# Raw weight tiles of the attention part are issued by GpSimd instead of SyncE

## The chip, the core and the metric

The kernel runs on one of the eight cores of a Trainium2 chip. A core has five engines with instruction queues of their own: TensorE (PE) for matrix products, VectorE (DVE), ScalarE (ACT), GpSimd (POOL), and SyncE (SP), which here only issues transfers. Sixteen DMA engines move data between HBM and the on-chip memory. The metric is device time in microseconds (us) of one execution. Before the change the median of three runs is 503.27 us (502.56 to 503.57).

## The reference

Three parts follow one another, all in float32. B = 2, 12 heads, 448 positions, head size 64; 896 tokens with 768 columns.

```python
scores = q @ k.T / 8;  scores = where(mask, -1e9, scores)      # causal
attn = exp(scores - max) / (sum(exp(scores - max)) + 1e-9)
x = (attn @ v)              # laid out as 896 tokens x 768
h = maximum(maximum(x @ w1, x @ w2), x @ w3)                   # 768 x 768 each
x = h @ w_out                                                  # 768 x 768
g = s * relu(x @ w_in) ** 2 + b                                # 768 x 2048
out = g @ w_out2                                               # 2048 x 768
```

## The kernel before

**Number format.** TensorE multiplies in a reduced format. Every operand is therefore split in a high and a low part (HL for q and k, x, h and g for the activations, whi and wlo for the weights), and a product is three products.

**Weights.** All four weight matrices lie in HBM as 56 tiles of 128 rows by 768 values of 8 bytes (768 KB each). A raw tile (wraw) is asked for by `fetch_w` (line 125), into one of three buffers. It is decoded in stages: ScalarE reads its two halves ("high" and "low", lines 144 and 147), VectorE clamps, shifts, sets the sign and adds (lines 153 to 179), ScalarE rounds to whi (line 184), VectorE forms wlo (line 92). "sign" is the last reader of the raw tile. For tiles decoded behind the attention, "sign" also asks for the next raw tile; for the first four (`tiles`, NT_AHEAD = 4) it doesn't, so the raw tiles of the attention part are asked for by explicit calls in the steps.

**Attention.** Twelve pairs of heads are worked on in a pipeline of 14 steps (`step(s)`, s = 0 to 13). The order of the work is written out by hand, and each engine executes its instructions in that order. In step s, with new = s and old = s - 1:

- TensorE forms masks and scores of pair `new` (mask_a, mask_b, mask_c, scores; lines 350 to 388) in the banks A, B and C, transposes the exponentials of pair `old` (line 435), and multiplies pair s - 2 with v (pv, lines 451 to 460) into the one bank o.
- VectorE finds row minima (mx), ScalarE exponentials (p).
- The row sums of `old` are inverted, transposed by TensorE into a corner of bank A of the new pair (line 480), copied out by VectorE (rows, line 487), written to HBM by SyncE in two parts (rcd, lines 488 and 489) and read back as a broadcast in two halves (rb, line 497). The mask product of the next step writes bank A again, so it comes after the copy of rows.
- VectorE multiplies o with rb for pair s - 3 (xf, line 506). That empties bank o, and the next pv may begin. GpSimd makes x from xf (lines 296 and 92).
- q and k of pair s + 2 are split: VectorE casts (HL from R, line 309), GpSimd subtracts (HL, line 92) and copies the last columns (bd, line 296). R of pair s + 3 is scaled by GpSimd beforehand (`scaled`, line 296), and the cast needs that.
- SyncE loads R of pair s + 4 (line 268) and pieces of v (line 289): V_LOADS[s] gives how many ahead of the broadcast of rb and how many behind it.
- Raw weight tiles: the branch `else: fetch_w()` runs where there is no old pair, that is in steps 0 and 13, and `if s in FETCH` in steps 1, 4, 8, 10 and 11. Each is in SyncE's queue.

A transfer instruction waits in the queue of the engine that issues it, and what stands behind it in that queue waits too.

**After the attention** TensorE runs through the products of the other two parts (lines 698 and 807) while the weights are decoded ahead. The output is stored in two halves of the columns (line 825), seven stores each, in SyncE's queue between the last loads of raw tiles.

Of the kernel before, what the change touches and what calls it, by code (L numbers as in the profile page):

```python
# [26 lines left out]
FETCH = (1, 4, 8, 10, 11)  # L27
# [9 lines left out]
    12: ("hi2", "low3"),  # L37
}
V_GROUPS = ((0, 1), (1, 1), (2, 4), (6, 6))
V_LOADS = ((7, 7), (2, 5), (3, 4), (3, 0), (3, 0), (3, 0), (3, 0), (2, 0))  # L40
FILL = {12: (3, 5), 13: (0, 4)}
WARM = 10
BUSY = (7,)
# [7 lines left out]
def kernel(  # L51
# [14 lines left out]
    nc = tc.nc  # L66
# [55 lines left out]

    step = begin

    def fetch_w():
        if w_src:
            src = w_src.pop(0)
            raw = wr_p.tile([128, DM], I64, tag="wraw", name="wraw")
            nc.sync.dma_start(out=raw, in_=src)
            raws.append(raw)  # L130

    def decoder(over=None, fetch=fetch_w):


# [97 lines left out]
    def attention():  # L232
        with ExitStack() as c2:
# [52 lines left out]
            def load_v(n):  # L286
                for _ in range(min(n, len(v_list))):
                    to, of = v_list.pop(0)
                    nc.sync.dma_start(out=to, in_=of)  # L289
# [5 lines left out]
            def pool_scaled(out, in_, by):  # L295
                nc.gpsimd.tensor_scalar(
                    out=out, in0=in_, scalar1=by, scalar2=1.0, op0=ALU.mult, op1=ALU.mult
                )
# [4 lines left out]
            def scaled(p):  # L303
                q = pair[p]["R"][:, 0, :]
                pool_scaled(q, q, -scale)

            def split_hi(p):
                new_hl(p)
                nc.vector.tensor_copy(out=pair[p]["HL"][:, 0:4:2, :], in_=pair[p]["R"])  # L309

            def split_lo(p):
                HL, R = pair[p]["HL"], pair[p]["R"]
                for n in range(2):
                    sub_lo(nc.gpsimd, HL[:, 2 * n + 1], R[:, n], HL[:, 2 * n])
# [7 lines left out]
            def split_lo_early(p):  # L322
                HL, R = pair[p]["HL"], pair[p]["R"]
                nc.vector.scalar_tensor_tensor(
                    out=HL[:, 1], in0=R[:, 0], scalar=-scale, in1=HL[:, 0].bitcast(F32),
                    op0=ALU.mult, op1=ALU.subtract,
                )
                sub_lo(nc.vector, HL[:, 3], R[:, 1], HL[:, 2])
# [13 lines left out]
            def both_tails(p):  # L342
                HL = pair[p]["HL"].bitcast(F32)
                for h in range(2):
                    pool_scaled(bds[p % 3][hs[h], :, hs[h]], HL[hs[h], 0:2, TAIL:S], 1.0)
# [47 lines left out]
            def minima(p, i):  # L393
                e = pair[p]
                src, cols = (at(p, i), slice(2 * i, 2 * i + 2)) if i < NQ else (e["C"][:, 0:S], slice(2 * NQ, 2 * NQ + 1))
                nc.vector.tensor_reduce(
                    out=e["mx"][:, cols], in_=src, axis=mybir.AxisListType.X, op=ALU.min
                )
# [40 lines left out]
            def pt_copy(p, n, eng):  # L439
                copy = eng.copy if eng is nc.scalar else eng.tensor_copy  # L440
                copy(out=pair[p]["PT"][:, n * 512:(n + 1) * 512], in_=pair[p]["t", n])
# [50 lines left out]
            def broadcast(p):  # L492
                e = pair[p]
                flat = e["flat"]
                for h in range(2):
                    at = h * (NQ + 1) * 128
                    nc.sync.dma_start(
                        out=e["rb"][hs[h]], in_=flat[:, at:at + S].to_broadcast([D, S])
                    )
# [17 lines left out]
            for p in range(1, 4):  # L517
# [6 lines left out]
                out=tri.rearrange("p (a n) -> p a n", a=2), in_=tri.rearrange("p (a n) -> p a n", a=2), pattern=[[0, 2], [-1, TQ]], base=0, channel_multiplier=1,  # L524
# [26 lines left out]
            def step(s):  # L551
                new, old, out, nxt = (
                    p if 0 <= p < n_pairs else None for p in (s, s - 1, s - 2, s + 2)
                )
                loads = V_LOADS[s] if s < len(V_LOADS) else (0, 0)
                if new is not None:
# [31 lines left out]
                if new == 0:  # L588
                    for i in (0, 1, 2, NQ):
                        minima(new, i)  # L590
                    split_lo_early(1)
                    both_tails(1)
                    for n in (2, 3):
                        scaled(n)
                    for V in vs[:2]:
                        nc.gpsimd.memset(V[D:128, :, :, NQ, :], 0.0)
                elif new is not None:
                    minima(new, 2)
# [53 lines left out]
                if old is not None:  # L652
                    load_v(loads[0])
                    broadcast(old)
                else:
                    fetch_w()
                load_v(loads[1])
                if s in FETCH:
                    fetch_w()
                if s == LAST:  # L660
                    nc.sync.dma_start(out=sb[:, 0:1], in_=s2.to_broadcast([128, 1]))
                    nc.sync.dma_start(out=sb[:, 1:2], in_=b2.to_broadcast([128, 1]))
                if new == 1:
                    split_hi(nxt)
                    split_lo(nxt)
                    both_tails(nxt)
                    scaled(s + 3)
                if old is not None:
                    pt_copy(old, 2, nc.scalar)
                if new is not None:  # L670
# [11 lines left out]
            for s in range(n_pairs + 2):  # L682
                step(s)
# [196 lines left out]
```

## Time and profile before

| | us |
|---|---|
| median of three runs | 503.27 |
| profiled execution | 502.06 |
| its span in the trace | 500.3 |
| TensorE busy | 493.3 (99%) |
| VectorE busy | 340.5 (68%) |
| ScalarE busy | 282.9 (57%) |
| GpSimd busy | 71.4 (14%) |

The busy tenths in 40 slices of 12.5 us show where each engine works; GpSimd works in the attention part alone:

```profile
PE   8999999999999999999999999999999999999997
DVE  5778896665857667587677888888888644484401
ACT  5988977444445254444546878888786432253101
POOL 6988992300000000000000000000000000000000
DMA  5777534223324231333223323332333323261003
```

A share of the whole span says little about one stage: the 14% of GpSimd are 80% and more in slices 2 to 6. Issues of transfers aren't counted as busy. Every wait in the timelines carries, in brackets, how long the engine idled and what ended it.

### The profile page before, as it was taken

The numbers are of one execution on the slowest core, as the hardware profiler recorded it, in microseconds if no ns is written. First come the engines' busy times: TensorE is split into PE (matmuls) and PEld (weight loads), VectorE is DVE, ScalarE is ACT, GpSimd is POOL, SyncE is SP. The second block draws the span as 40 slices with busy tenths as digits, with TensorE's granted clock in tenths as the row PEclk, the third lists the DMA queues.
The fourth block names the chain that finished last, engine by engine and source line by source line (L and its number), as shares of the span: only waits on it lengthen the run. The fifth ranks groups of instructions, "written<-read, shape, count | busy, mean of one in ns | idle before, by whom it ended". The sixth has DMA issues, their size and how long they took to land.

```text
span 500.3 us, 7557 instructions
## 1 busy us (share of the span) xinstructions
PE 493.3 (99%) x2909; PEld 452.7 (90%) x2909; DVE 340.5 (68%) x512; ACT 282.9 (57%) x527; POOL 71.4 (14%) x103
## 2 busy tenths in 40 slices
PE   8999999999999999999999999999999999999997
PEld 4877888899999999999999999999999999999996
DVE  5778896665857667587677888888888644484401
ACT  5988977444445254444546878888786432253101
POOL 6988992300000000000000000000000000000000
PEclk9999999999999999999999999999999999999999
DMA  5777534223324231333223323332333323261003
GB/s 170 225 215 226 151 102 117 103 91 127 126 75 148 94 126 64 126 128 126 101 89 126 127 73 118 126 104 85 127 126 109 119 89 128 88 220 56 1 0 111
DMA packets 26212, 58.34 MB, mean 117 GB/s; under 512 B 13548, under 2 KB 17600, under 8 KB 26176
## 3 DMA queue, kind: packets, MB, share of 16 engines
q1 hardware_dynamic: 26032, 57.76, 35.2%
q8 instruction: 23, 0.38, 0.3%
q14 instruction: 13, 0.11, 0.1%
q10 hardware_dynamic: 144, 0.10, 0.1%
HBM read 55.05 MB, written 2.80 MB: 116 GB/s over the span
## 4 chain that ended last, share of the span: by engine, by line
PE 91%; DMA 2%; DVE 2%; SPq 2%; ACT 1%; POOL 1%; issue 0%; DVEq 0%; ACTq 0%
PE m L698 58%; PE m L807 23%; PE t L435 3%; PE o L451 2%; ACT p L408 1%; PE o L455 1%; SPq L289 1%; PE A L380 1%; PE C L388 1%; PE B L380 1%; DMA rcd<-rows 1%; DMA rb<-rcd 1%; DMA R<-in_qk_dram 1%; POOL HL L92 0%; PE o L460 0%
## 5 line engine op out<-in xcount | busy, mean ns | idle before, releaser
L698 PE MATMUL m<-x,whi 128*128 128x448 f32 x816 | 232.0, 366 | 0.0
L698 PEld LDWEIGHTS m<-x,whi 128*128 128x128 f32 x816 | 153.1, 188 | 12.3 <-ACT p L408 0.2
L698 PE MATMUL m<-x,wlo 128*128 128x448 f32 x408 | 149.0, 365 | 0.0
L807 PE MATMUL m<-whi,g 128*128 128x384 f32 x448 | 114.0, 334 | 0.0
L184 ACT CAST whi<-wa 128x768 fp32r<-128x768 f32 x56 | 46.7, 833 | 67.0 <-PE m L807 43.8
L698 PEld LDWEIGHTS m<-x,wlo 128*128 128x128 f32 x408 | 76.6, 188 | 6.0
L807 PEld LDWEIGHTS m<-whi,g 128*128 128x128 f32 x448 | 81.0, 188 | 0.0
L144 ACT ACTIVATE wa<-wraw 128x768 f32<-128x768 f32 x56 | 50.6, 904 | 52.3 <-DVE wlo L92 52.3
L92 DVE TENSOR_TENSOR wlo<-wa,whi 128x768 fp32r<-128x768 f32 x56 | 53.3, 953 | 38.4 <-ACT whi L184 38.4
L807 PE MATMUL m<-wlo,g 128*128 128x384 f32 x224 | 74.8, 334 | 0.0
L179 DVE CUSTOM_DVE_ANT_0 wa<-wa,wr 128x1536 uint16<-128x1536 uint16 x56 | 53.6, 957 | 1.9
L172 DVE SCALAR_TENSOR_TENSOR wa<-wraw,wa 128x768 int32<-128x768 int32 x56 | 53.7, 959 | 0.0
L147 ACT ACTIVATE wr<-wraw 128x768 int32<-128x768 uint32 x56 | 50.6, 904 | 0.0
L807 PEld LDWEIGHTS m<-wlo,g 128*128 128x128 f32 x224 | 42.0, 188 | 0.0
L705 DVE TENSOR_TENSOR t<-t,m 128x448 f32<-128x448 f32 x24 | 14.9, 621 | 38.7 <-PE m L698 38.7
L698 PE MATMUL m<-h,whi 128*128 128x448 f32 x144 | 40.9, 365 | 0.0
L166 DVE TENSOR_SCALAR wa<-wa 128x768 int32<-128x768 int32 x56 | 32.2, 575 | 1.8
L92 POOL TENSOR_TENSOR HL<-R,HL 128x448 fp32r<-128x448 f32 (+1 forms) x21 | 29.9, 1443 | 3.2 <-DVE HL L309 2.1
L792 ACT ACTIVATE r<-m 128x448 f32<-128x448 f32 x32 | 17.4, 544 | 22.2 <-PE m L698 22.2
L698 PEld LDWEIGHTS m<-h,whi 128*128 128x128 f32 x144 | 27.1, 188 | 2.1
L158 DVE TENSOR_SCALAR wa<-wa 128x768 f32<-128x768 f32 x52 | 28.7, 552 | 0.0
L781 DVE SCALAR_TENSOR_TENSOR r<-m,r 128x448 f32<-128x448 f32 x32 | 20.0, 625 | 12.3 <-ACT r L792 12.3
(85 smaller groups left out, 551.2 us busy)
## 6 DMA issues: line engine op xcount, KB each, us to landing
wraw<-in_w_dram SPq DMA_DIRECT2D x56, 768.0 KB
R<-in_qk_dram SPq DMA_DIRECT2D x11, 448.0 KB
rb<-rcd SPq DMA_DIRECT2D x24, 112.0 KB
out_dram<-o SPq DMA_DIRECT2D x13, 192.0 KB
v<-in_v_dram SPq DMA_DIRECT2D x4, 96.0 KB
v<-in_v_dram SPq DMA_DIRECT2D x2, 168.0 KB
v<-in_v_dram SPq DMA_DIRECT2D x6, 48.0 KB
v<-in_v_dram SPq DMA_DIRECT2D x2, 144.0 KB
```

The lines of the kernel that those rows point to most:

```text
L92: eng.tensor_tensor(out=lo, in0=full, in1=hi.bitcast(F32), op=ALU.subtract)
L144: nc.scalar.activation(out=e["f"], in_=e["high"].bitcast(F32), func=ACTF.Abs)
L147: nc.scalar.activation(out=e["r"], in_=e["low"].bitcast(U32), func=ACTF.Copy, scale=2.0 ** -29)
L158: nc.vector.tensor_scalar(out=e["f"], in0=e["f"], scalar1=UNDER, scalar2=OVER, op0=ALU.max, op1=ALU.min)
L166: nc.vector.tensor_scalar(out=a, in0=a, scalar1=3, scalar2=0x3FFFFFF8, op0=ALU.logical_shift_left, op1=ALU.bitwise_and,)
L172: nc.vector.scalar_tensor_tensor(out=e["a"], in0=e["high"], scalar=-0x40000000, in1=e["a"], op0=ALU.bitwise_and, op1=ALU.bitwise_or,)
L179: nc.vector.tensor_tensor(out=e["a"], in0=e["a"], in1=e["r"], op=ALU.add)
L184: nc.scalar.copy(out=e["hi"], in_=e["f"])
L698: nc.tensor.matmul(p, wt[w][:, ws], cols(act[i], a, b), start=(i == 0 and n == 0), stop=(i == len(act) - 1 and n == 2),)
L781: nc.vector.scalar_tensor_tensor(out=r, in0=p, scalar=0.0, in1=r, op0=ALU.max, op1=ALU.mult)
L792: after(0, lambda: nc.scalar.activation(out=r, in_=p, func=ACTF.Relu))
L807: nc.tensor.matmul(acc[t][:, 0:EH], gt[f][:, a, ts], w[:, ws], start=(f == 0 and n == 0), stop=(f == KG - 1 and n == 2),)
```

## The change

`fetch_w` takes the queue as an argument. In the attention part the raw tiles are now asked for in GpSimd's queue: in step 0 behind the scaling of pairs 2 and 3, in steps 1, 4, 8, 10 and 11 behind the step's own scaling. The branch that ran in steps 0 and 13 is gone, so that six raw tiles instead of seven are asked for in the steps. Of the v pieces behind rb one moves from step 2 to step 1: (2, 5), (3, 4) becomes (2, 6), (3, 3). "sign" goes on asking in SyncE's queue.

```diff
--- before.py
+++ after.py
@@ -37,7 +37,7 @@
     12: ("hi2", "low3"),
 }
 V_GROUPS = ((0, 1), (1, 1), (2, 4), (6, 6))
-V_LOADS = ((7, 7), (2, 5), (3, 4), (3, 0), (3, 0), (3, 0), (3, 0), (2, 0))
+V_LOADS = ((7, 7), (2, 6), (3, 3), (3, 0), (3, 0), (3, 0), (3, 0), (2, 0))
 FILL = {12: (3, 5), 13: (0, 4)}
 WARM = 10
 BUSY = (7,)
@@ -122,11 +122,11 @@
 
     step = begin
 
-    def fetch_w():
+    def fetch_w(queue=nc.sync):
         if w_src:
             src = w_src.pop(0)
             raw = wr_p.tile([128, DM], I64, tag="wraw", name="wraw")
-            nc.sync.dma_start(out=raw, in_=src)
+            queue.dma_start(out=raw, in_=src)
             raws.append(raw)
 
     def decoder(over=None, fetch=fetch_w):
@@ -592,6 +592,7 @@
                     both_tails(1)
                     for n in (2, 3):
                         scaled(n)
+                    fetch_w(nc.gpsimd)
                     for V in vs[:2]:
                         nc.gpsimd.memset(V[D:128, :, :, NQ, :], 0.0)
                 elif new is not None:
@@ -652,11 +653,7 @@
                 if old is not None:
                     load_v(loads[0])
                     broadcast(old)
-                else:
-                    fetch_w()
                 load_v(loads[1])
-                if s in FETCH:
-                    fetch_w()
                 if s == LAST:
                     nc.sync.dma_start(out=sb[:, 0:1], in_=s2.to_broadcast([128, 1]))
                     nc.sync.dma_start(out=sb[:, 1:2], in_=b2.to_broadcast([128, 1]))
@@ -665,6 +662,8 @@
                     split_lo(nxt)
                     both_tails(nxt)
                     scaled(s + 3)
+                if s in FETCH:
+                    fetch_w(nc.gpsimd)
                 if old is not None:
                     pt_copy(old, 2, nc.scalar)
                 if new is not None:
```

GpSimd's queue in steps 0 to 2, before: R is the scaling, HL the split, bd the copy of last columns, v a memset of v's unused rows.

```order
L296 TENSOR_SCALAR R<-R 128x448 x2
L596 MEMSET v_112 64x2x64
L596 MEMSET v_113 64x2x64
L92 TENSOR_TENSOR HL<-R,HL 128x448 x2
L296 TENSOR_SCALAR bd_109<-HL 64x2x64 x2
L606 MEMSET v_114 64x8x64
L606 MEMSET v_115 64x12x64
L92 TENSOR_TENSOR HL<-R,HL 128x448 x2
L296 TENSOR_SCALAR bd_107<-HL 64x2x64 x2
L296 TENSOR_SCALAR R<-R 128x448
L92 TENSOR_TENSOR HL<-R,HL 128x448 x2
```

The same place in the changed kernel:

```order
L296 TENSOR_SCALAR R<-R 128x448 x2
L129 DMA wraw<-in_w_dram 128x768
L597 MEMSET v_112 64x2x64
L597 MEMSET v_113 64x2x64
L92 TENSOR_TENSOR HL<-R,HL 128x448 x2
L296 TENSOR_SCALAR bd_109<-HL 64x2x64 x2
L607 MEMSET v_114 64x8x64
L607 MEMSET v_115 64x12x64
L92 TENSOR_TENSOR HL<-R,HL 128x448 x2
L296 TENSOR_SCALAR bd_107<-HL 64x2x64 x2
L296 TENSOR_SCALAR R<-R 128x448
L129 DMA wraw<-in_w_dram 128x768
```

A load now stands behind the scaling of pairs 2 and 3 and one behind the scaling of pair 4, each ahead of a split.

SyncE's queue in steps 1 to 3, before, from the first pieces of v behind the broadcast of step 1:

```order
L289 DMA v_114<-in_v_dram 16x4x64 x2
L289 DMA v_114<-in_v_dram 96x4x64 x2
L289 DMA v_114<-in_v_dram 32x4x64
L129 DMA wraw<-in_w_dram 128x768
L488 DMA rcd<-rows 7x128
L489 DMA rcd<-rows 1x64
L268 DMA R<-in_qk_dram 128x896
L289 DMA v_114<-in_v_dram 32x4x64
L289 DMA v_114<-in_v_dram 80x4x64 x2
L497 DMA rb<-rcd 64x448 x2
L289 DMA v_114<-in_v_dram 48x4x64 x2
L289 DMA v_114<-in_v_dram 64x4x64 x2
```

The same place in the changed kernel:

```order
L289 DMA v_114<-in_v_dram 16x4x64 x2
L289 DMA v_114<-in_v_dram 96x4x64 x2
L289 DMA v_114<-in_v_dram 32x4x64 x2
L488 DMA rcd<-rows 7x128
L489 DMA rcd<-rows 1x64
L268 DMA R<-in_qk_dram 128x896
L289 DMA v_114<-in_v_dram 80x4x64 x2
L289 DMA v_114<-in_v_dram 48x4x64
L497 DMA rb<-rcd 64x448 x2
L289 DMA v_114<-in_v_dram 48x4x64
L289 DMA v_114<-in_v_dram 64x4x64 x2
```

The raw tile ahead of rcd is gone, one piece of v (32 rows) has moved ahead of rcd, and three instead of four pieces stand between the broadcast of step 2 and the next rcd.

SyncE's queue at the end, before, from the last broadcast on (out_dram is the output):

```order
L497 DMA rb<-rcd 64x448 x2
L129 DMA wraw<-in_w_dram 128x768 x47
L825 DMA out_dram<-o 128x384 x7
L129 DMA wraw<-in_w_dram 128x768 x3
L825 DMA out_dram<-o 128x384 x6
L819 DMA out_dram<-o 128x192
```

The same place in the changed kernel:

```order
L497 DMA rb<-rcd 64x448 x2
L129 DMA wraw<-in_w_dram 128x768 x46
L824 DMA out_dram<-o 128x384 x7
L129 DMA wraw<-in_w_dram 128x768 x4
L824 DMA out_dram<-o 128x384 x6
L818 DMA out_dram<-o 128x192
```

One load, the 53rd of the 56, has moved behind the seven stores of the first half.

## Rows read from the trace of the kernel before

**Rows 1.** Busy by stretch: us, PE PEld DVE ACT POOL, clock, DMA share, GB/s.

```profile
21.88:28.26 6.38, 6.38 (x67) 5.31 (x66) 5.91 (x11) 6.27 (x21) 6.14 (x8) 1.00 0.86 256
28.26:35.86 7.60, 6.52 (x68) 5.36 (x66) 5.60 (x11) 6.22 (x20) 5.73 (x8) 1.00 0.57 146
35.86:43.10 7.24, 6.46 (x67) 5.33 (x65) 5.71 (x11) 6.21 (x20) 5.87 (x8) 1.00 0.92 222
43.10:49.49 6.39, 6.39 (x67) 5.32 (x65) 5.38 (x11) 6.05 (x20) 6.14 (x8) 1.00 0.74 238
```

**Rows 2.** Timeline of VectorE, products with rb: start, us, what, idle before.

```profile
32.21 0.62 DVE L506 TENSOR_TENSOR xf<-o,rb 128x448 f32<-128x448 f32 x1 [1.64 <-DMA rb<-rcd]
...
39.53 0.62 DVE L506 TENSOR_TENSOR xf<-o,rb 128x448 f32<-128x448 f32 x1 [1.33 <-DMA rb<-rcd]
```

**Rows 3.** Chain of waits, steps 2 and 3: start, us, what.

```profile
21.01 0.63 DVE HL L309
21.64 0.18 DVE rows L487
...
23.07 3.99 DMA rcd<-rows
...
28.89 1.78 SPq L289
```

**Rows 4.** Timeline of SyncE's DMA issues.

```profile
22.57 0.41 SPq L129 DMA_DIRECT2D wraw<-in_w_dram  x1
...
24.15 1.54 SPq L289 DMA_DIRECT2D v<-in_v_dram  x3
27.12 1.09 SPq L497 DMA_DIRECT2D rb<-rcd  x2
28.26 3.77 SPq L289 DMA_DIRECT2D v<-in_v_dram  x4
32.13 0.45 SPq L488 DMA_DIRECT2D rcd<-rows  x1
...
62.24 0.25 SPq L489 DMA_DIRECT2D rcd<-rows  x1
63.11 1.09 SPq L497 DMA_DIRECT2D rb<-rcd  x2
...
435.96 3.58 SPq L825 DMA_DIRECT2D out_dram<-o  x7
```

**Rows 5.** Timeline of GpSimd, steps 0 to 5, with idle time and its end.

```profile
11.03 1.09 POOL L296 TENSOR_SCALAR R<-R 128x448 f32<-128x448 f32 x2
...
20.41 0.56 POOL L296 TENSOR_SCALAR R<-R 128x448 f32<-128x448 f32 x1
21.79 3.03 POOL L92 TENSOR_TENSOR HL<-R,HL 128x448 fp32r<-128x448 f32 x2 [0.81 <-DVE HL L309]
...
32.92 0.56 POOL L296 TENSOR_SCALAR x<-xf 128x448 fp32r<-128x448 f32 x1 [1.00 <-DVE xf L506]
...
40.24 0.56 POOL L296 TENSOR_SCALAR x<-xf 128x448 fp32r<-128x448 f32 x1 [0.50 <-DVE xf L506]
...
42.66 3.05 POOL L92 TENSOR_TENSOR HL<-R,HL 128x448 fp32r<-128x448 f32 x2 [0.63 <-DVE HL L309]
...
46.42 0.56 POOL L296 TENSOR_SCALAR R<-R 128x448 f32<-128x448 f32 x1
```

**Rows 6.** Timeline of TensorE, first mask product of step 3.

```profile
21.88 0.27 PE L350 MATMUL A<-tri,identb 128*128 128x128 bf16 x2
```

**Rows 7.** Timeline of VectorE, step 6.

```profile
47.29 0.70 DVE L309 CAST HL<-R 128x896 fp32r<-128x896 f32 x1
48.82 0.28 DVE L487 COPY rows<-A 7x128 f32<-7x128 f32 x1 [0.83 <-PE A L480]
```

**Rows 8.** Timeline of ScalarE, second output half.

```profile
442.51 0.91 ACT L144 ACTIVATE wa<-wraw 128x768 f32<-128x768 f32 x1 [1.06 <-DVE wlo L92]
...
445.86 0.84 ACT L184 CAST whi<-wa 128x768 fp32r<-128x768 f32 x1 [1.63 <-PE m L807]
```

## Prediction

> **What bounds the kernel now.** I read the busy table by stretches first, then the chain of waits, then the timelines of the engines that the chain passes. A step of the twelve pairs, from one mask product to the next, lasts 6.38 or 6.39 us where TensorE never stops, but 7.60 us in step 4 and 7.24 us in step 5 [rows 1]. So TensorE bounds a step, and what anything else can give back in the pairs is mainly 1.21 + 0.85 = 2.06 us. VectorE names the cause in both steps: it stands 1.64 us in step 4 and 1.33 us in step 5 until the broadcast reciprocals rb have landed [rows 2], and TensorE's next product with v waits for the bank that VectorE then empties. The chain goes back from there through SyncE: rcd was written out at 23.07 and took 3.99 us [rows 3]. In SyncE's queue a raw weight tile was issued just ahead, at 22.57 [rows 4]. In step 9, with no load and no piece of v near, rcd's second part was issued at 62.24 and the broadcast that needs it at 63.11, so it landed within 0.62 us [rows 4]. The second wait starts earlier still: rb of step 2 went out only at 27.12 although SyncE had finished the pieces of v before it at 25.69; four more pieces, in 3.77 us, held the next rcd until 32.13 [rows 4].
>
> The chain has a second place, and it speaks against the change. GpSimd's rows from 11.03 to 20.97 name no idle time, and VectorE's cast of pair 4 starts at 21.01, right behind GpSimd's scaling of pair 4, then VectorE copies the reciprocals' row out until 21.82, and TensorE's mask product of step 3, which writes the same bank, starts at 21.88 [rows 3, 5, 6]. Whatever is put into GpSimd's queue before 20.41 moves TensorE by as much.
>
> **What the change does, part by part.** It takes six loads out of SyncE's queue (0.41 us of issue each, [rows 4]), a seventh disappears from step 13, and six go into GpSimd's: one ahead of all of step 0's later GpSimd work, one behind the scaling of pair 4, one each in steps 4, 8, 10 and 11.
>
> *The waits for rb.* If the raw tile no longer stands ahead of rcd, it lands before SyncE is done with the pieces of v, and the broadcast of step 2 goes out at about 25.7, 1.4 us earlier. That covers what step 4 needs: 1.64 us less the delay that VectorE gets below. Behind that broadcast three pieces of v remain instead of four, at 3.77 / 4 = 0.94 us each, so the next rcd and its broadcast come 1.4 + 0.94 = 2.3 us earlier, more than the 1.33 us that step 5 waited. Both waits go: -2.06 us. What is late next there is TensorE itself.
>
> *The first GpSimd issue.* The trace has no DMA issued by GpSimd. From below, an issue costs what the same load costs on SyncE, 0.41 us [rows 4]; nothing would make it less, since the row of GpSimd is only lengthened. From above I take the longest issue of the stretch, 1.78 us on SyncE [rows 3]. GpSimd's own nearest rows are passes over 448 columns at 0.55 us (1.09 for two) and splits at 1.5 us (3.03 for two) [rows 5]; I take the middle of the bounds, 1.1 us, which lies between these. It passes whole to TensorE in step 3: +1.1 us. TensorE's own later start also hides nothing, because VectorE's copy of the row comes at 21.82 and the mask product at 21.88 [rows 3, 6].
>
> The Trainium skill weighs on this price in "DMA: Bandwidth & Descriptors", Specifications: the first byte of a transfer issued by GpSimd comes after about 1 us, against 0.6 us for SyncE. By it as an estimate the sum would be 2.06 - 1.0, a gain of 1.06 us; no row here shows it.
>
> *The second and third issue.* Call an issue's cost d. GpSimd has little room: from step 1 to its scaling of pair 8, which ends at 46.98, it idles 0.81, 1.00, 0.50 and twice 0.63 us (one of these two shown), 3.57 us in all [rows 5]. Three issues fall before that point, so pair 8 is scaled at the earliest at 46.98 + 3d - 3.57. VectorE's cast of pair 8 starts at 47.29, 0.31 us behind it; VectorE then idles 0.83 us before its row copy at 48.82, which ends at 49.10, 0.39 us before the mask product at 49.49 [rows 1, 5, 7]. So GpSimd may be 0.31 + 0.83 + 0.39 = 1.53 us late before TensorE ends later than now. Two terms compete: change = the larger of d - 2.06 and 3d - 5.10. They cross at d = 1.52. At 1.1 the second gives -1.8, and GpSimd's room still hides the two later issues. Cover gone, each 0.1 us of d costs 0.3.
>
> *The loads in GpSimd's queue in steps 8, 10 and 11.* Their waits are for buffers whose last reader ran a step or more before; behind them stand the splits of pair 11 and of finished pairs. I cost them at nothing beside the 1.5 us of room just named; bound 0 to d for the one in step 8, the last with a split for the scores behind it.
>
> *The load missing from step 13.* Every load is then asked for by the tile before in the same buffer, so its start, set by the release of that buffer, stays. But the order in SyncE's queue shifts by one: 52 loads instead of 53 stand ahead of the seven stores of the first output half. The shifted one goes out after the stores, at 435.96 + 3.58 = 439.54 [rows 4]. ScalarE reads it at 442.51, idles 1.63 us soon after for TensorE, and splits of later tiles wait for TensorE in turn [rows 8]. I cost it at nothing, hidden by tiles decoded ahead; if it landed later than 442.51 + 1.63 = 444.14, the next split would move, and only after that margin is used would TensorE.
>
> **The sum.** -2.06 + 1.1 = -0.96 us. The profiled execution took 502.06 us (span 500.3 and 1.76 around it), so the like of it would take 501.10. The median of the runs before is 503.27, 1.21 above that execution; the same 0.96 off it gives 502.3.
>
> **Rivals.**
>
> *The bytes decide, not the queue.* The same load runs at the same time beside rcd, rb and R; the stretch of step 5 moves 222 GB/s and step 6, without a wait, 238 [rows 1]. If rb lands no sooner, VectorE's 1.64 and 1.33 us stay as absolute times, the delay of 1.1 is swallowed by the first of them, and the time is 503.3. Against it: 3.99 us beside 0.62 for the same small write is the mark of standing behind something in order. The Trainium skill sides with this rival ("DMA: Bandwidth & Descriptors", Issuing engines are not separate DMA queues): transfers of all issuing engines run on the same 16 DMA engines, and another issuer saves only the issue time. By it the gain would be six issues of 0.41 us off SyncE's queue alone.
>
> *GpSimd becomes the bound (slower).* Its place is the scaling of pair 8 ahead of VectorE's cast, the price 3d - 5.10, and it decides from d = 1.70. At d = 2.2 the time is 503.27 + 1.5 = 504.8. For it: GpSimd's split took 3.03 us at 21.79 and would take two passes of less were VectorE idle; it has no idle rows in step 0. Against it: 2.2 is above every DMA issue in the rows.
>
> *An issue waits out a cast.* VectorE's cast of 0.63 us lies right where the second issue would run [rows 3]. If each issue stands still through one, d = 1.1 + 0.63 = 1.73, and 3d - 5.10 gives +0.1: 503.4. The Trainium skill has this as a rule ("SBUF — State Buffer", SBUF: two separate sides): GpSimd can't write descriptors while VectorE runs a pass that takes both ports. Its example is 3.1 us beside a copy, which as an estimate would make +4.2 us; no row here shows a DMA from GpSimd.
>
> *More is regained.* The runs' median stands 1.21 us above the profiled execution; if that is longer waits for the same rb, they go too: 502.3 - 1.2 = 501.1.
>
> **How the numbers follow.** Forecast 0.52 (its own range, d from 0.41 to 1.70: 501.6 to 503.3), bytes 0.13, cast 0.10, GpSimd as bound 0.20, more regained 0.05. A measurement of this kernel can tell 0.2%, 1.0 us, from no change. Faster by more: 0.38 of the forecast (d below 1.06 or a little luck of the runs) and 0.05, 0.43 in all. Within: 0.14 of the forecast, 0.13 and 0.10, 0.37. Slower: 0.20. The range for 8 in 10 is 501.2 to 504.4: it takes in most of d from 0.41 to 2.07 and leaves out the far ends of both sides.
>
> **What would show it.** Right: steps 4 and 5 last 6.4 us; VectorE's products with rb name no DMA; step 2 of TensorE, to the mask product at 21.88, ends about 1.1 us later; GpSimd's rows show a gap of some 1.1 us where the issues are; from step 6 all is about 1 us earlier to the end. Wrong: VectorE still waits for rb (bytes); casts of pairs 8 to 11 wait for GpSimd's scaling and the steps are longer than 6.4 us (GpSimd as bound); ScalarE waits for a DMA near 442.

## The result, and the profile after

The changed kernel takes 505.1 us (median of 20 runs, 502.82 to 511.13) against 502.52 us before (20 runs in the same batch): ratio 1.0052, 95% interval 1.0039 to 1.0065. The longest run, 511.13 us, is left out of the ratio. The kernel is slower by about 2.6 us; the forecast was 502.3 us, 0.96 us under the 503.27 of the first three runs.

The profiled execution took 504.58 us, its span is 502.8 us: 2.5 more than before. Three places make that up. TensorE's first mask product starts at 10.67 us instead of 10.03 (+0.64). From there to the long run of products behind the attention it takes 84.52 us instead of 83.08 (+1.44). That run and what follows last the same up to the issue of the last store (497.61 and 499.69 us); behind it the span has 0.42 us more. Of the 1.44 us, steps 4 to 6 make 0.69, read below, and steps 8 and 9 make 0.83 (6.65 and 6.98 us instead of 6.42 and 6.38).

The table of busy times by stretch, for the same four steps as [rows 1] (us, PE, PEld, DVE, ACT, POOL, clock, DMA share, GB/s):

```profile
22.48:28.87 6.39, 6.39 (x67) 5.33 (x65) 5.91 (x11) 6.33 (x21) 6.14 (x8) 1.00 0.91 264
28.87:35.26 6.39, 6.39 (x67) 5.33 (x65) 5.73 (x11) 6.13 (x20) 5.52 (x8) 1.00 0.55 148
35.26:42.33 7.07, 6.47 (x68) 5.31 (x65) 5.81 (x11) 6.23 (x20) 6.16 (x9) 1.00 0.96 231
42.33:50.79 8.46, 6.44 (x67) 5.31 (x65) 5.96 (x11) 6.13 (x20) 6.21 (x8) 1.00 0.66 192
```

Step 4 lasts 6.39 us instead of 7.60: that part came in this execution. Step 5 keeps 7.07 of 7.24. Step 6, which had no wait, now takes 8.46 us: what step 4 gave back is lost there, and more. VectorE's products with rb, the answer to [rows 2], say by whom:

```profile
31.49 0.62 DVE L506 TENSOR_TENSOR xf<-o,rb 128x448 f32<-128x448 f32 x1 [0.28 <-DMA rb<-rcd]
...
38.74 0.62 DVE L506 TENSOR_TENSOR xf<-o,rb 128x448 f32<-128x448 f32 x1 [1.16 <-DMA rb<-rcd]
...
47.22 0.62 DVE L506 TENSOR_TENSOR xf<-o,rb 128x448 f32<-128x448 f32 x1 [2.50 <-DMA rb<-rcd]
```

The chain of waits through step 6 (start, us, what) goes back to the broadcast itself:

```profile
35.58 3.27 DMA rcd<-rows
...
38.93 0.54 SPq L497
...
39.57 7.55 DMA rb<-rcd
...
47.22 0.64 DVE xf L506
...
47.90 0.54 PE o L451
```

The chain of the kernel before holds one broadcast of this kind, in step 5:

```profile
35.60 3.84 DMA rb<-rcd
```

So one rb takes 7.55 us where another took 3.84. The timeline of GpSimd shows what began just before it (the DMA rows are the issues of the raw tiles; this answers to [rows 5]):

```profile
11.80 0.75 POOL L129 DMA_DIRECT2D wraw<-in_w_dram  x1
...
13.58 2.24 POOL L92 TENSOR_TENSOR HL<-R,HL 128x448 fp32r<-128x448 f32 x2 [0.64 <-DVE HL L309]
...
21.52 0.84 POOL L129 DMA_DIRECT2D wraw<-in_w_dram  x1
...
39.16 0.60 POOL L129 DMA_DIRECT2D wraw<-in_w_dram  x1
```

An issue costs GpSimd 0.60 to 0.84 us. Step 4's load leaves at 39.16; in SyncE's queue it left behind both broadcasts (41.23 before). The view of the DMA engines over the time that this rb takes (39.6 to 47.1 us; q0 is GpSimd's queue, q1 SyncE's):

```profile
DMA packets 2196, 1.95 MB, mean 260 GB/s; under 512 B 1797, under 2 KB 1932, under 8 KB 2194
...
q1 hardware_dynamic: 2050, 1.14, 59.1%
q0 software_dynamic: 144, 0.79, 33.6%
```

and over the 3.84 us of the kernel before (35.6 to 39.4 us):

```profile
DMA packets 1664, 0.89 MB, mean 234 GB/s; under 512 B 1443, under 2 KB 1578, under 8 KB 1664
```

The rates are alike, the bytes are not. The load's 0.79 MB at 260 GB/s are 3.0 us, most of the 3.7 us by which rb got longer.

The same is seen at the first wait. GpSimd issued step 1's load at 21.52, but the broadcast of step 2 still went out at 27.43 (27.12 before, [rows 4]), 4.38 us behind its rcd (4.05 before). The timeline of SyncE:

```profile
23.05 0.29 SPq L488 DMA_DIRECT2D rcd<-rows  x1
...
27.43 1.10 SPq L497 DMA_DIRECT2D rb<-rcd  x2
...
77.06 0.27 SPq L488 DMA_DIRECT2D rcd<-rows  x1
...
81.18 1.11 SPq L497 DMA_DIRECT2D rb<-rcd  x2
```

From 23.1 to 27.4 us the DMA engines carry all 144 packets of that load, though it was issued 1.6 us earlier:

```profile
DMA packets 687, 1.28 MB, mean 298 GB/s; under 512 B 442, under 2 KB 449, under 8 KB 687
...
q0 software_dynamic: 144, 0.79, 53.8%
q1 hardware_dynamic: 543, 0.49, 38.3%
```

The clearest case is step 10, with no piece of v near. Its rcd leaves at 77.06 and its broadcast at 81.18, 4.12 us later, since the load that GpSimd issued at 76.37 runs in between. No wait of TensorE follows from it in this trace, so it shows the cause and not the price. In the kernel before the two were 1.18 us apart (SyncE's timeline):

```profile
74.95 0.27 SPq L488 DMA_DIRECT2D rcd<-rows  x1
...
76.13 1.11 SPq L497 DMA_DIRECT2D rb<-rcd  x2
```

The Trainium skill, "DMA: Bandwidth & Descriptors", Issuing engines are not separate DMA queues, says that transfers of all issuing engines run on the same 16 DMA engines and interleave, and that a second issuer saves only issue time. The first half agrees with these rows: in one view q0 and q1 take 33.6% and 59.1% of the engines' time, and two queues move 260 GB/s where one moved 234. The second half leaves out what the rows show: 4.12 us instead of 1.18 for a row of reciprocals, because the order of one queue was lost.

In the output stage ScalarE now waits for the load that moved behind the stores (its timeline, the answer to [rows 8]):

```profile
445.96 0.91 ACT L144 ACTIVATE wa<-wraw 128x768 f32<-128x768 f32 x1 [2.44 <-DMA wraw<-in_w_dram]
...
447.94 0.84 ACT L184 CAST whi<-wa 128x768 fp32r<-128x768 f32 x1 [0.27 <-PE m L806]
```

The next split still waits for TensorE, whose last run of products lasts 116.00 us in both kernels: this costs nothing.

### The profile page after: what moved, and what is told of

Same layout as the page of the kernel before. It is cut to its first block, busy times and chain, and to the rows that moved or that the text cites. A ratio compares the mean times of both kernels' runs of the same rounds, so it can differ in the third digit from the quotient of the medians.

```text
span 502.8 us, 7570 instructions
## 1 busy us (share of the span) xinstructions
PE 494.0 (98%) x2909; PEld 453.2 (90%) x2909; DVE 341.9 (68%) x512; ACT 282.8 (56%) x527; POOL 73.7 (15%) x109
## 4 chain that ended last, share of the span: by engine, by line
PE 93%; DMA 2%; DVE 2%; ACT 2%; issue 0%; SPq 0%; ACTq 0%; DVEq 0%
PE m L697 58%; PE m L806 23%; PE t L435 3%; PE o L451 2%; DMA rb<-rcd 2%; ACT p L408 1%; PE B L380 1%; PE o L455 1%; PE A L380 1%; PE C L388 1%; DVE mx L396 1%; PE warm L513 1%; DMA rcd<-rows 1%; PE B L358 1%; PE o L460 0%
## 5 line engine op out<-in xcount | busy, mean ns | idle before, releaser
L92 POOL TENSOR_TENSOR HL<-R,HL 128x448 fp32r<-128x448 f32 (+1 forms) x21 | 28.8, 1391 | 4.2 <-DVE HL L309 2.5
```

Of the source, the lines that this page charges most:

```text
L92: eng.tensor_tensor(out=lo, in0=full, in1=hi.bitcast(F32), op=ALU.subtract)
```

## Experiments

The theory under test: **order of bytes**. In the pairs the DMA engines are near full where v and raw tiles move (DMA share 0.91 and 0.96 in steps 3 and 5 above). A load in a second queue is served along with SyncE's transfers, so it takes its 3 us ahead of rcd or rb, which it had followed in SyncE's order. Rivals: GpSimd's issue time; GpSimd's queue as such; the new order of v.

Ratios are to the kernel before, run in the same batch. In the expectations, rcd and rb of step 0, 1, 2 or 3 are those of that pair, which SyncE issues one step later. Where a diff uses `fetch_w(nc.gpsimd)`, `fetch_w` takes the queue as in the change.

**Step 4's load back on SyncE.**

```diff
 # changed kernel
                 load_v(loads[1])
+                if s == 4:
+                    fetch_w()
-FETCH = (1, 4, 8, 10, 11)
+FETCH = (1, 8, 10, 11)
```

> The changed kernel with step 4's load back in SyncE's queue behind rb; the other five loads stay with GpSimd. Theory of shared turns (a load in another queue takes turns with SyncE's packets on the DMA engines, so rb of step 4, which stood ahead of the load, is stretched): the 2.0 us wait of TensorE in step 6 goes, the time is about 2 us under the changed kernel, ratio to before 0.998 to 1.001. Rival, GpSimd's own issue time: one issue of 0.6 us less, ratio about 1.004. Rival, the order of v pieces: no change, 1.005.

Measured: 1.0042 (1.0024 to 1.006). Step 6 is 6.39 us again, as expected, but the time hardly fell: the expectation missed it. The chain of waits has the same loss in another place. GpSimd issued a load at 80.80, right on the broadcast:

```profile
75.20 4.46 DMA rcd<-rows
...
80.19 5.91 DMA rb<-rcd
```

TensorE waits 1.66 us behind this broadcast. In the changed kernel the same load left at 82.65, 0.36 us after SyncE was done issuing that broadcast (81.18 to 82.29), and TensorE did not wait there. So a later load can do what step 4's did, and a few tenths of a microsecond may decide whether it does.

**Step 4's load alone on GpSimd**, all else as before.

```diff
 # kernel before
-                if s in FETCH:
+                if s in FETCH and s != 4:
                     fetch_w()
 ...
                     scaled(s + 3)
+                if s == 4:
+                    fetch_w(nc.gpsimd)
```

> The kernel before with step 4's load alone in GpSimd's queue. Shared turns: rb of step 4 takes some 7 us instead of 3.8 and TensorE waits about 2 us in step 6, ratio 1.003 to 1.005. GpSimd's issue time: GpSimd idles 0.50 us at that place, so at most 0.1 us, ratio 1.000.

Measured: 1.0088 (1.0064 to 1.0112; six runs), more than expected. Beside the waits of steps 4 and 5 (0.80 and 0.81 us), TensorE now waits 3.16 us in step 6; chain and TensorE's timeline:

```profile
41.24 7.51 DMA rb<-rcd
```

```profile
49.52 0.59 PE L451 MATMUL o<-PT,v 128*64 128x448 f32 x1 [3.16 <-DVE xf L506]
```

One load in another queue costs some 4 us: 4.4 by the ratio, 3.7 by the medians.

**GpSimd's time alone.** The kernel before, with a fill of 640 columns on GpSimd at each of the six places; all loads stay with SyncE.

```diff
 # kernel before
                         scaled(n)
+                    nc.gpsimd.memset(idle, 0.0)
 ...
                     scaled(s + 3)
+                if s in FETCH:
+                    nc.gpsimd.memset(idle, 0.0)
```

> The kernel before with a memset of 640 columns (about 0.7 us) in GpSimd's queue at the six places where the changed kernel issues loads; all loads stay in SyncE's queue. Shared turns: only what GpSimd delays, 0 to 0.7 us, ratio 1.000 to 1.0015. GpSimd's issue time as the cause: the whole loss, ratio 1.004 to 1.005.

Measured: 0.9999 (0.9985 to 1.0012). GpSimd's issue time isn't the cause. It does reach TensorE: step 2 lasts 7.72 us instead of 6.99, and the mask product of step 3 waits for VectorE's copy (TensorE's timeline). Steps 4 and 5 then last 6.37 and 6.46 us, with next to no wait for rb: the delay is swallowed there.

```profile
23.16 0.27 PE L351 MATMUL A<-tri,identb 128*128 128x128 bf16 x2 [0.67 <-DVE rows L488]
```

**Step 4's load on ScalarE's queue.**

```diff
 # kernel before
-                if s in FETCH:
+                if s in FETCH and s != 4:
                     fetch_w()
 ...
                 decode(END.get(s, ()))
+                if s == 4:
+                    fetch_w(nc.scalar)
```

> The kernel before with step 4's load alone in ScalarE's queue, issued at about the time at which the changed kernel issues it. Shared turns: any second queue does it, so TensorE waits about 2 us in step 6, ratio 1.003 to 1.005. Rival, something of GpSimd's queue alone (descriptors written by software): no wait in step 6, ratio 1.000 to 1.001 (ScalarE's issue of some 0.4 us).

Measured: 1.0048 (1.0023 to 1.0073). Not GpSimd's queue as such, then. The load left at 37.31, and this time it was the pieces of v ahead of rb that it held in SyncE's queue. SyncE took 4.96 us to issue the three (1.87 before), and the chain goes from them back to the landing of the raw tile; why a piece of v waits for it is not shown. SyncE's timeline and the chain:

```profile
38.73 4.96 SPq L289 DMA_DIRECT2D v<-in_v_dram  x3
```

```profile
37.31 6.04 DMA wraw<-in_w_dram
...
45.45 2.81 DMA rb<-rcd
```

**Step 4's load on SyncE, ahead of the broadcasts.** One queue, one place earlier.

```diff
 # kernel before
                     load_v(loads[0])
+                    if s == 4:
+                        fetch_w()
                     broadcast(old)
 ...
-                if s in FETCH:
+                if s in FETCH and s != 4:
```

> The kernel before with step 4's load still in SyncE's queue, but one place earlier: ahead of the two broadcasts of step 3's reciprocals instead of behind them. Shared turns, as a matter of place in time: the load's bytes are taken before or along with rb's wherever they are issued, so TensorE waits 1.5 to 3.5 us in step 6: ratio 1.003 to 1.008. Rival, it takes a second queue (one queue serves its transfers so that the small one is not delayed by the load ahead): no wait above 0.5 us in step 6, ratio 0.999 to 1.001.

Measured: 1.0041 (1.0024 to 1.0058), and TensorE waits 2.55 us in step 6, both as expected. The chain:

```profile
39.45 0.93 SPq L129
...
41.41 6.96 DMA rb<-rcd
```

Without any second queue rb takes 6.96 us. So the place ahead of rb is what costs; a second queue is one way of getting there.

**Step 4's load on GpSimd, two microseconds later.**

```diff
 # kernel before, FETCH without step 4
                     pv_out(s - 3)
+                if s == 5:
+                    fetch_w(nc.gpsimd)
```

> The kernel before with step 4's load alone on GpSimd, as in the run that gave 1.0088, but issued about 2 us later, ahead of GpSimd's split in step 5, at some 41 to 42 us instead of 39.4, behind the first broadcast of step 3 (issued at 39.7). Shared turns: rb is then mostly through, or shares only its end: it lands within 4 to 5.5 us instead of 7.5, TensorE waits 0 to 1.5 us in step 6 instead of 3.16: ratio 0.999 to 1.005, clearly under 1.0088. Rival, GpSimd's queue is slow whatever the moment: the wait stays near 3 us and the ratio near 1.009. Rival, GpSimd's time counts: the split comes 0.7 us later and TensorE waits 0.3 to 0.7 us more in step 6.

Measured: 1.0008 (0.9992 to 1.0023). Issued at 41.55, behind both broadcasts, the load costs nothing measurable; step 6 lasts 6.40 us. Same queue, same bytes, another moment: 1.0008 instead of 1.0088. SyncE's and GpSimd's timelines:

```profile
39.20 1.67 SPq L497 DMA_DIRECT2D rb<-rcd  x2
```

```profile
41.55 0.75 POOL L129 DMA_DIRECT2D wraw<-in_w_dram  x1
```

**Half of it on GpSimd.**

```diff
 # kernel before, step 4
+            nc.sync.dma_start(out=raw[64:128, :], in_=src[64:128, :])   # behind rb
 ...
+            nc.gpsimd.dma_start(out=raw[0:64, :], in_=src[0:64, :])     # GpSimd's place
```

> The kernel before with the raw tile of step 4 in two halves of 64 partitions: one from GpSimd at the changed kernel's place, one from SyncE behind the broadcasts, where the whole stood. Shared turns by bytes: half the bytes run beside rb, so the wait in step 6 falls from 3.16 us to 0.5 to 2 us; ratio 1.001 to 1.005. Rival, any transfer of a second queue holds rb for its issue or its first packets, whatever its size: wait near 3 us, ratio near 1.009.

Measured: 1.0032 (1.0013 to 1.0051), within the range of the dose, but the profiled execution, among the longest of its runs, shows TensorE waiting 2.79 us in step 6 and one rb taking 7.68 us, as beside a whole load. Median and trace disagree; this one is inconclusive.

**Steps 8, 10 and 11 alone on GpSimd.**

```diff
 # kernel before
-                if s in FETCH:
+                if s in (1, 4):
                     fetch_w()
 ...
+                if s in (8, 10, 11):
+                    fetch_w(nc.gpsimd)
```

> The kernel before with only the loads of steps 8, 10 and 11 on GpSimd, at the changed kernel's places; steps 0, 1 and 4 stay with SyncE. Shared turns: the loads start just ahead of rcd in steps 10 and 11, and the broadcast goes out some 4 us behind rcd instead of 1.2; the waits of steps 4 and 5 stay (1.2 and 0.85 us). Where the stretch from step 9 to the products of the steady part has slack (step 12 and the tail of the pairs), this costs 0 to 2 us: ratio 1.000 to 1.004. Rival, only step 4's load matters: ratio 0.999 to 1.001 and the steady products start at 93.1 to 93.4 us, as before.

Measured: 1.002 (1.0007 to 1.0033), as expected. In its trace TensorE waits nowhere behind the loads of steps 10 and 11; its one long wait, 1.68 us in step 5, lies ahead of all three. So the trace does not show where the 0.2% goes. The gap from rcd to its broadcast is 3.94 us instead of 1.18 (SyncE's timeline):

```profile
76.08 0.27 SPq L488 DMA_DIRECT2D rcd<-rows  x1
...
80.02 1.11 SPq L497 DMA_DIRECT2D rb<-rcd  x2
```

**Only steps 0 and 1 on GpSimd**, with the new order of v.

```diff
 # changed kernel
                 load_v(loads[1])
+                if s in FETCH and s > 1:
+                    fetch_w()
 ...
-                if s in FETCH:
+                if s == 1:
                     fetch_w(nc.gpsimd)
```

> The changed kernel, but the loads of steps 4, 8, 10 and 11 go back to SyncE's queue behind the broadcasts; only those of steps 0 and 1 stay with GpSimd, and the pieces of v stay in the new order. Shared turns (a load in a second queue takes turns with rcd and rb, which it followed in order before): steps 6 to 12 have no wait for rb beyond those of the kernel before; step 4's wait of 1.2 us is gone, about 0.6 us of step 5's remains, so about 1 us is gained: ratio to before 0.998 (0.996 to 1.000). Rival, the new order of v costs: step 5 still waits more than 1 us of TensorE and the ratio is above 1.000. Rival, the phase of GpSimd and VectorE (in step 9 of the changed kernel two of VectorE's passes took 1.21 and 1.30 us, before 0.54 and 1.09, and TensorE waited 0.52 us): step 9 shows that wait here too, and the ratio is 0.999 to 1.001.

Measured: 1.0008 (0.9994 to 1.0023). The part of the change on which the forecast's gain rested brings none. The third rival's wait is there (0.60 us in step 9), but also in runs with all loads on SyncE (0.53 with the fills), so these loads are not its cause. The profiled execution is the longest of its runs; in it rb of step 2 leaves 5.5 us behind its rcd (SyncE's timeline):

```profile
25.11 0.28 SPq L488 DMA_DIRECT2D rcd<-rows  x1
...
30.60 2.21 SPq L497 DMA_DIRECT2D rb<-rcd  x2
```

**The order of v alone.**

```diff
-V_LOADS = ((7, 7), (2, 5), (3, 4), (3, 0), (3, 0), (3, 0), (3, 0), (2, 0))
+V_LOADS = ((7, 7), (2, 6), (3, 3), (3, 0), (3, 0), (3, 0), (3, 0), (2, 0))
```

> The kernel before with only the new order of the pieces of v: one of step 2's goes a step sooner, ahead of the load in SyncE's queue; all loads stay with SyncE. Shared turns: one piece more (0.94 us, 3.77 for four) stands ahead of step 1's rcd and one less ahead of step 2's: step 4's wait grows by up to 0.9 us and step 5's shrinks by as much; the sum is near nothing: ratio 0.999 to 1.001, and no wait in step 6. Rival, the order of v is the cause of the slow result: ratio 1.003 or more.

Measured: 0.9996 (0.9985 to 1.0007). It is not the cause. Steps 4 and 5 last 7.02 and 6.94 us; the expected shift from one to the other does not show.

**Step 1's load alone on GpSimd.**

```diff
 # kernel before
-                if s in FETCH:
+                if s in FETCH and s != 1:
                     fetch_w()
 ...
+                if s == 1:
+                    fetch_w(nc.gpsimd)
```

> The kernel before with only step 1's load on GpSimd, at the changed kernel's place behind the scaling of pair 4; the others and the order of v as before. Turns theory: issued about 21.5 us it is served in turns with the pieces of v that stand ahead of rcd, so rcd lands about when it did, the next broadcast goes out at 27.0 to 27.6 (27.12 before), and the waits of steps 4 and 5 together stay within 0.6 us of before's 1.86 us: ratio 0.999 to 1.002. Rival, the forecast's step: the load out of SyncE's order lets rcd land first; that broadcast goes out at 25.7 to 26.2, both waits go: ratio 0.996 to 0.998.

Measured: 0.9995 (0.9982 to 1.0008). The broadcast goes out at 27.18, not at 25.7, and 4.38 us behind rcd where it was 4.05: the forecast's step fails even by itself (SyncE's timeline). Steps 4 and 5 wait less than expected, they last 6.61 and 7.04 us, but TensorE's first mask product came 1.00 us later in this execution (11.03).

```profile
22.80 0.29 SPq L488 DMA_DIRECT2D rcd<-rows  x1
...
27.18 1.10 SPq L497 DMA_DIRECT2D rb<-rcd  x2
```

**Step 1's load ahead of the five pieces of v**, same queue.

```diff
 # kernel before
+                if s == 1:
+                    fetch_w()
                 load_v(loads[1])
-                if s in FETCH:
+                if s in FETCH and s != 1:
```

> The kernel before with step 1's load a few places earlier in SyncE's queue: behind the broadcast of step 0 and ahead of the five pieces of v that it followed. The sum of bytes ahead of rcd is the same. Turns theory: rcd lands when it did, the broadcast goes out at 26.9 to 27.4, waits as before: ratio 0.999 to 1.001. Rival, what stands directly ahead counts: the broadcast goes out at 26.5 or sooner and step 4's wait shrinks by 0.5 us or more: ratio 0.997 to 0.999.

Measured: 1.0029 (1.0014 to 1.0044); neither expectation had that. SyncE issued the load at 20.38, rcd at 23.58 and the broadcast only at 28.30, and step 4 lasts 8.21 us. The chain shows what held the broadcast: SyncE stood 1.9 us at the load of R behind rcd until the raw tile had landed (20.38 + 5.95 = 26.33), and the pieces of v and the broadcast came after. In the kernel before R left at 23.75, right behind rcd.

```profile
20.38 5.95 DMA wraw<-in_w_dram
...
26.39 0.36 SPq L268
```

Why the load of R waits for the raw tile is not shown.

**Step 1's load later in SyncE's queue**, in step 2 and in step 3.

```diff
-FETCH = (1, 4, 8, 10, 11)
+FETCH = (2, 4, 8, 10, 11)    # the first
+FETCH = (3, 4, 8, 10, 11)    # the second
```

> The kernel before with the load of step 1 moved to step 2 in SyncE's queue, behind the four pieces of v there and ahead of rcd of step 2. Place theory: step 4's wait of 1.2 us shrinks by 0.4 us or more, step 5's of 0.85 us grows by as much or more, since four pieces and the load stand ahead of its rcd: ratio 0.999 to 1.003. Rival, the load's place does not matter among the pieces of v: both waits as before and ratio 1.000.

> The kernel before with the load of step 1 moved to step 3 in SyncE's queue, behind that step's broadcast; nothing on GpSimd. The load no longer stands ahead of rcd of step 1: step 4's wait of 1.2 us shrinks to 0.3 us or less. It now stands ahead of rcd of step 3, which TensorE needs in step 6, where rb had slack: 0 to 1.5 us of wait there. Place theory: ratio 0.997 to 1.001, a better kernel if step 6 has room. Rival, waits for rb are regained elsewhere and only change their step: ratio 0.999 to 1.001. Rival, decoding stands for its missing tile: ScalarE or VectorE wait for a raw tile in steps 3 to 5 and the ratio is above 1.001.

Measured: 1.006 (1.0034 to 1.0087) and 1.0164 (1.0145 to 1.0183). The rival named for step 3 took both: the tile is needed there. ScalarE's timeline in the first and in the second, and TensorE's in the second:

```profile
34.15 0.90 ACT L144 ACTIVATE wa<-wraw 128x768 f32<-128x768 f32 x1 [4.06 <-DMA wraw<-in_w_dram]
```

```profile
40.92 0.89 ACT L144 ACTIVATE wa<-wraw 128x768 f32<-128x768 f32 x1 [11.37 <-DMA wraw<-in_w_dram]
```

```profile
42.99 0.38 PE L480 MATMUL A<-ident,su 128*7 128x128 f32 x1 [9.07 <-ACT p L408]
```

ScalarE decodes in the order that was written out, so its exponentials stand behind the missing tile.

**Step 1's load in step 0 on SyncE**, twice, and once with the new order of v added.

```diff
 # kernel before
                 else:
                     fetch_w()
+                    if s == 0:
+                        fetch_w()
-FETCH = (1, 4, 8, 10, 11)
+FETCH = (4, 8, 10, 11)
```

> The kernel before with step 1's load issued in step 0, right behind step 0's own, both ahead of that step's pieces of v in SyncE's queue; nothing on GpSimd. Its bytes are then taken ten us earlier and none of a load runs beside rcd of step 1. Turns theory: the next broadcast goes out 0.4 to 1.4 us earlier than 27.12 unless the pieces of v, now behind a second load, are pushed back by as much; waits of steps 4 and 5 together 0.5 to 1.9 us: ratio 0.997 to 1.001. Rival, the bytes of a stretch decide wherever they stand: the queue is full from step 0 to step 6, so the delay is only handed on: rcd of step 0 comes later, TensorE's waits keep their sum, ratio 1.000 to 1.003.

> The same kernel as the run that gave 0.9985 (0.9974 to 0.9997), measured once more on its own. If that was a gain: ratio 0.9975 to 0.9995, below 1 with its interval. Rival, it was luck of the runs: ratio 0.9995 to 1.001.

> Step 1's load in step 0 on SyncE, as in the run that gave 0.9985, and with it the changed kernel's order of the pieces of v; nothing on GpSimd. If both edits that harmed nothing add up: ratio 0.997 to 0.9995, rcd of step 2 issued about 1 us earlier than in that run (32.34) and step 5's wait of 0.88 us shrunk to 0.4 us or less. Rival, the bytes of the stretch decide: what step 5 gains step 4 loses, ratio 0.998 to 1.000, no better than without it.

Measured: 0.9985 (0.9974 to 0.9997), then 1.0007 (0.9988 to 1.0027); with the order of v 0.9991 (0.9976 to 1.0007). The small gain did not come again. In the first of them the broadcast of step 2 left 2.58 us behind its rcd (4.05 before), but both left late enough (25.08 and 27.66) that steps 4 and 5 kept 6.90 and 7.33 us: the delay was handed on. In the second the gap is 2.59 us, and the steps last 7.63 and 6.38 us. With the order of v step 5 still waits 0.72 us, not 0.4 or less. No version here is shown to beat the kernel before; the best are the same as it.

## Why the prediction was wrong

By its own steps:

- **What bounds the kernel** (TensorE, with 2.06 us lost to rb in steps 4 and 5): right for that execution, too much taken from it. One kernel profiled twice (step 1's load in step 0) has 6.90 and 7.33 us in them once, 7.63 and 6.38 the other time. And the waits take up what is late ahead of them: with fills step 2 lasts 0.73 us longer, and steps 4 and 5 last 6.37 and 6.46 us at the same total time. In seven profiles of kernels that are alike up to step 4 the first mask product starts at 9.93 to 10.94 us and step 6 at 42.68 to 43.50, and steps 4 and 5 are shortest together (13.89 us) where the start is latest. In the changed kernel step 6 starts at 42.33 (43.10 before) from a start 0.64 us later. The two waits of one trace were priced as if every execution paid them and nothing else would fill in.
- **The waits for rb, -2.06 us** ("it lands before SyncE is done with the pieces of v, and the broadcast of step 2 goes out at about 25.7"): failed. It went out at 27.43, and at 27.18 with that load moved alone. Leaving the queue does not leave the DMA engines: the 0.79 MB ran from 23.1 to 27.4 beside rcd. Step 4 gained 1.21 us in this execution and step 5 only 0.17; steps 0 and 1 with the order of v gave 1.0008 over the runs. Where the bytes really were gone (step 1's load in step 0) rcd and its broadcast came 1.5 us closer, as the forecast had it, and still the time did not fall; rcd itself left 2.0 us later.
- **The first GpSimd issue, +1.1 us**: d was 0.60 to 0.84, inside the bounds. In this execution it did not pass to TensorE: GpSimd idles 0.64 us for VectorE at 13.58 behind the first issue, and step 2 lasts 6.94 us against 6.99 before. With the fills it passed as forecast (7.72 us in step 2), but the later waits took it up, so the two terms of the sum could not be added.
- **The second and third issue, hidden by GpSimd's room**: right.
- **The loads in steps 8, 10 and 11, and in step 4, at nothing**: this is the step that made the sign wrong. It looked at what stands behind the load in GpSimd's queue, and not at what the load had stood behind in SyncE's: rcd and rb. Out of that order it goes ahead of them in time. Step 4's alone costs 1.0088 and the other three 1.002. Together they cost less than their sum (1.0052 in all). In the changed kernel step 4's load makes TensorE wait 2.02 us, alone 3.16, and no wait stands behind the later ones. Why it costs less in company is not shown; the run with step 4's load back on SyncE suggests that a shift in one step changes which broadcast a later load meets.
- **The load missing from step 13**: right; the margin of 1.63 us was used, and TensorE did not wait.
- **Rivals.** "The bytes decide, not the queue" had the mechanism. I gave it 0.13 and a time of 503.3, for I asked only whether the old waits stay and not whether the same bytes, now earlier, make new ones. The argument against it was misread: 3.99 us run from the issue of rcd, 0.62 us from the end of its second part's issue. Alike, from rcd's issue to the broadcast's, they are 4.05 and 1.18 us (step 9, rcd at 61.93), and bytes in flight explain that as well as an order in a queue. "GpSimd becomes the bound" had the sign, and was not it: the chain holds rb at step 6, no scaling. Its time of 504.8 was near the result for another reason. No issue waited out a cast at its price (0.84 us at most).

What is left of the profiled difference: +0.64 us ahead of the first mask product, where the start varies (9.93 to 11.03 us over the profiles of this study), is not traced to the change; nor are the 0.83 us of steps 8 and 9, which runs without a load on GpSimd show as well (6.81 and 6.98 us with the fills). So the step 4 load is shown to be harmful, by its own runs; how the 2.6 us of the whole change divide is not shown.

## What to carry to other kernels

A queue is also a priority: a large load that stands behind a small transfer on the critical path is held back by it, and in a queue of its own it no longer is. Before moving a transfer, list what it follows as well as what follows it, and price it by its bytes at the rate that the stretch already moves (here 0.79 MB at 260 GB/s, 3 us), not by its issue. A wait in one trace is worth its length only if other executions show it too, and if nothing that is late ahead of it would use it up.

## What the runs showed of the hardware

A GpSimd issue of 768 KB in 128 rows took 0.60 to 0.84 us in the changed kernel, against 0.41 to 0.58 for SyncE in the pairs of the kernel before, and the tile landed 4.5 to 7.6 us after it.

In three runs SyncE stood, by the releasers that the profile infers, at a transfer until an earlier raw tile had landed, though no data pass between the two: 1.9 us at a load of R (step 1's load ahead of v), 3.3 us at a piece of v (step 4's load on ScalarE) and 2.5 us at a piece of v (step 4's load ahead of the broadcasts). No run tested why.

The span of the kernels with loads on GpSimd ends later behind the issue of the last store, by the rounded spans: 2.7 us before, 2.8 to 2.9 with one or two such loads, 3.0 with three and with five, 3.1 with six. No run tested why.
